# Top-k attention and mixture of depths on one core: score blocks turned by half rows, and a new order of signs, exponentials and loads

## The chip, the core and the metric

The kernel runs on one core of one Trainium2 chip. The metric is the device time in microseconds of one execution; a version is represented by the median of several runs. Engines are called by the names that the profile gives them: PE (matrix products; PEld is its loading of weights), DVE (VectorE), ACT (ScalarE), POOL (GpSimd) and SP (which here only issues DMAs).

## What is computed

Two operators follow one another. The first is attention with 8 batches, 8 heads, 576 tokens and 64 elements a head, in which each row keeps only its 32 largest scores:

```python
scores = scale * np.matmul(q, k.transpose(0, 1, 3, 2))
kth = np.partition(scores, -top_k, axis=-1)[..., -top_k:-top_k + 1]
scores = np.where(scores >= kth, scores, -1000000000.0)
attn = softmax(scores)            # over the keys
x = np.matmul(attn, v)            # then heads side by side: (8, 576, 512)
```

The second, the mixture of depths, works on each batch: a gate `x @ w_gate` for every token, and for the 128 tokens with the largest gates `x + sigmoid(gate) * (relu(x @ w1) @ w2)`, with w1 of 512 x 1024; all other tokens keep x.

## The kernel before

**Units and steps.** Work is cut into 144 units, 18 to a batch. A unit is 128 query rows of two heads; the last 64 rows of a batch are laid out so that four heads share one unit. One pass of the loop at L1108 is called a step here. It is a software pipeline written out by hand: step n computes the scores of unit n + 1, finds a bound for unit n, the signs for unit n - 1, the exact threshold for unit n - 2, the mask for unit n - 3, and turns, exponentiates and multiplies unit n - 4 with the values. Each engine runs its instructions in the order in which the program issues them (`InOrder`, L37), so the order of the lines in the loop sets every queue.

**What a step does, engine by engine, in the order of the code.**

1. `weigh` (L1053) turns unit n - 4: `turn` (L621) takes the 128 x 576 scores of each of two heads in four blocks of 128 keys. For each of these eight blocks PE makes a transpose (a product with `ident`, FP32) into the PSUM tile `ptr` (two banks), and then adds a second product, of the 0/1 matrix `less` (BF16) with `out_of_reach` (a diagonal of very negative numbers), which pushes every score below the threshold out of the reach of the exponential. `turn_last` (L630) does the same for a ninth block, the last 64 keys of both heads together, into a corner of the PSUM bank `av`. Then ACT makes the exponentials: `pT` (128 x 1024) and `last` (128 x 128).
2. `mask_of` (L1102) makes `less` for unit n - 3: the first head on ACT, the second on POOL. `flush` issues small pieces of ACT work put off from the step before.
3. The scores of unit n + 1: first one or two load pieces (`load[0]`, transposes of rows of k and q for the next batch, whose issue also fetches a further piece by DMA on SP's queue), then `multiply` (L486): eight products of 64 x 128 weights and 288 columns into `ps` (four banks); the two heads lie on rows 0 to 63 and 64 to 127 of the array. ACT copies the load pieces (`load[1]`) and then the scores (`keep`, `sc`).
4. `values` (L642) multiplies `pT` and `last` with the values into the bank `av`; ACT copies the result (`xs`). Then follow, on PE, pieces of an earlier batch's mixture, which `next(mixtures[b])` issues at the end of a step at times listed by hand (`mix_at`, L1001).
5. DVE: `find_bound` (L520) takes the 8 largest of each of 14 pieces of a row and sifts them to a lower bound of the threshold. In the middle of it stand delayed pieces of work; `gates` makes the gate by a dot product (`prod`, 40 in all). Then `find_kth` (L573) takes the 8 largest of `y` (tile `next`), whose last is the exact threshold.
6. `what_is_below` (L1072), the last in the step: for each head ACT takes the sign of the score against the bound and sums it (`part`, L554, tile `sides`), POOL multiplies scores and signs (`y`), and `fill` adds 8 columns that depend on the count.

**Buffers.** There are five `sc`, two each of `sides`, `y`, `less` and `pT`, and one each of `ptr`, `av` and `ps`. PSUM has eight banks, all in use.

**After the loop** the last four units are weighed by `weigh_unit` and `values_unit` (L1241 to L1248) with more PSUM room, among the last batch's mixture. A general path at the end of the program, for inputs that the fast path can't treat, isn't entered here.

Of the kernel before, what the change touches and what calls it, by code (L numbers as in the profile page):

```python
# [48 lines left out]
def kernel(  # L49
# [160 lines left out]
    def flush():  # L210
        while late:
            late.pop(0)()
# [24 lines left out]
    class Rows:  # L237
# [88 lines left out]
        def turn(self, i, tr, c0=0, c1=J):  # L326

            for c in range(c0, c1):
                pe.transpose(
                    tr[:, c - c0, :],  # L330
                    self.rows[i][:, c, :, :].rearrange("p h d -> p (h d)"),
                    ident,
                )
            if c1 == J:
                self.fetch()
# [144 lines left out]
    def room_for_scores():  # L480
        return ps_sc.tile([P, 2, 2, 512], FP32, name="ps")
# [126 lines left out]
    def turn_some(tr, z, less):  # L608

        pe.transpose(tr, z, ident)  # L610
        if less is not None:
            pe.matmul(
                tr, less, out_of_reach, start=False, stop=True, skip_group_check=True
            )

    def room_to_turn():
        return ps_tr.tile([P, 2, J, P], FP32, name="ptr"), ps_av.tile(
            [P, 512], FP32, name="av"
        )

    def turn(z, tr, less=None):  # L621

        for i in range(2):
            for c in range(J):
                at = slice(c * P + i * R, (c + 1) * P + i * R)
                turn_some(
                    tr[:, i, c, :], z[:, i, at], None if less is None else less[:, i, at]
                )

    def turn_last(z, av, less=None):  # L630

# [10 lines left out]
    def values(t, g, pT, last, av, vs):  # L642

        vt, vpair = vs  # L650
        for i, heads in enumerate(heads_of(t, g)):
            for c in range(J):
                for r in (0, R):
                    h = heads[-1 if r else 0][0]
                    pe.matmul(
                        av[r : r + R, i * DE : (i + 1) * DE],
                        pT[:, i, c, r : r + R],
                        vt[:, h, c, :],
                        start=(c == 0 and i == 0),
                        stop=False,  # L660
                        skip_group_check=True,
                    )
        for r in (0, R):
            h = heads_of(t, g)[0][-1 if r else 0][0]
            pe.matmul(
                av[r : r + R, 0 : 2 * DE],
                last[:, r : r + R],
                vpair[:, h // 2, :, :].rearrange("p h e -> p (h e)"),
                start=False,
                stop=True,  # L670
                skip_group_check=True,
            )
# [373 lines left out]
    inverting = normalised = None  # L1046
    of_batch = {}
    scs, bounds, ys, next8s, masks = {}, {}, {}, {}, {}

    def is_unit(n):  # L1050
        return 0 <= n < N

    def weigh(sc, tr, av, less):  # L1053

        turn(sc, tr, less)
        tr_last = turn_last(sc, av, less)
        pT = ptpool.tile([P, 2, J, P], FP32, name="pT")
        last = ptpool.tile([P, P], FP32, name="last")

        def exp():  # L1060
            act.activation(pT, tr, AF.Exp, scale=scale)
            act.activation(last, tr_last, AF.Exp, scale=scale)

        return pT, last, exp

    def bound_of(n):
        b, i = divmod(n, per_batch)
# [2 lines left out]
        find_bound(scs[n], bounds[b][:, i, :, :])  # L1070

    def what_is_below(n):  # L1072
        at, sc = 2 * n, scs[n]
        b, i = divmod(n, per_batch)
        bound = bounds[b][:, i, :, :]
        sides = wkpool.tile([P, 2, S], BF16, name="sides")
        y = wkpool.tile([P, 2, S + 8], FP32, name="y")
        for i in range(2):
            part(i, sc, bound, at, sides)
            pool.tensor_tensor(y[:, i, 0:S], sc[:, i, :], sides[:, i, :], ALU.mult)  # L1080
        fill(y, at)
        ys[n] = y

    def kth_of(n):
# [23 lines left out]
    for n in range(-1, N):  # L1108
        b, i = divmod(n, per_batch)
        if i == 0 and 0 <= b < B - 1:  # L1110
            qkv[b + 1] = room_for_qkv(b + 1)
            loading = chain(
                loading, Rows(k[b + 1], q[b + 1], *qkv[b + 1][0:2]).parts()
            )
        if 0 < n + 1 < NHP:
            first_pairs.turn(n + 1)
        if n == 0:
            for hp in range(2):
                first_pairs.turn_queries(hp)
            for hp in range(2):  # L1120
                first_pairs.keep_queries(hp)
        if n == NHP - 1:
            for hp in range(2, NHP):
                first_pairs.turn_queries(hp)
            for hp in range(2, NHP):
                first_pairs.keep_queries(hp)
            first_pairs.last_queries()
            first_steps.close()
            ps_sc = all_steps.enter_context(
                tc.tile_pool(name="ps_sc", bufs=1, space=PS)  # L1130
            )
        if n == 1:
            load_v(v[0], qkv[0][2])
        if n == NHP:
            load_weights()


        gating = normalised
        if inverting is not None:
            normalised = inverting[0:2]  # L1140
            vector_late.insert(0, lambda a=inverting: normalise(*a))
            inverting = None
        else:
            normalised = None
        if gating is not None:
            amid_late.append(lambda a=gating: gates(*a))

        if is_unit(n - 4):  # L1150
            tr, av = room_to_turn()
            pT, last, exp = weigh(scs.pop(n - 4), tr, av, masks.pop(n - 4))
            exp()
        if is_unit(n - 3):
            mask_of(n - 3, (act, None) if n in scatter_steps else None)
        flush()
        if is_unit(n + 1):
            b, t, g = units[n + 1]
            kT, qT = qkv[b][0:2]
            b, i = divmod(n, per_batch)  # L1160
            if n + 1 < NHP:
                ps = room_for_first_scores()
                multiply(t, g, kT, qT, ps)
                if is_unit(n - 1):
                    what_is_below(n - 1)
                stay_busy((10, 10, 20, 30)[n + 1])
            else:
                ps = room_for_scores()
                loads = list(islice(loading, first_loads[i] if b == 0 else loads_at[i]))
                halves = [ps[:, a, :, HALF : HALF + P] for a in range(2)]  # L1170
                for load, half in zip(loads, halves):
                    load[0](half)
                multiply(t, g, kT, qT, by_head(ps))
                for load, half in zip(loads, halves):
                    load[1](half)
                if n == NHP - 1:
                    stay_busy(20)
            scs[n + 1] = keep(ps)
        if is_unit(n - 4):
            b4, t4, g4 = units[n - 4]  # L1180
            values(t4, g4, pT, last, av, qkv[b4][2])
            if n in place_steps:
                values_bank[0] = av
                next(mixtures[place_steps[n]])
            if g4 == 0:
                xs = xpool.tile([P, H, DE], FP32, name="xs")
                if t4 == 0:
                    x = xpool.tile([P, NT, HD], FP32, name="x")
                    pg = gates_of[b4 % 2]
                    of_batch[b4] = x, pg  # L1190
            keep_values(t4, g4, av, xs)
            if g4 == groups(t4) - 1:
                inverting = b4, t4, xs
                n4 = R if t4 == J else P
                keep_sums(n4, xs, sums[0:n4, b4 * NT + t4, :])
            while kept:
                kept.pop(0)()


        if is_unit(n):  # L1200
            bound_of(n)
        flush_vector()
        flush_pool()
        if is_unit(n - 2):
            kth_of(n - 2)
        while after_kth:
            after_kth.pop(0)()


        if is_unit(n - 1) and n + 1 >= NHP:  # L1210
            what_is_below(n - 1)

        if gating is not None:
            b, t = gating
            if t == J:
                store(out[b], of_batch[b][0])
                mixtures[b] = mixture(float(b * S), of_batch[b][1], ranks[:, b, :])
        for b in mix_steps.get(n, ()):
            next(mixtures[b], None)
        b, i = divmod(n, per_batch)  # L1220
        if i == v_at and 0 <= b < B - 1:
            load_v(v[b + 1], qkv[b + 1][2])
# [17 lines left out]

    def weigh_unit(m):  # L1241
        tr, av = other_room(m) if (N - m) % 2 else room_to_turn()
        weighed[m] = *weigh(scs.pop(m), tr, av, masks.pop(m)), av

    def values_unit(m):
        pT, last, _, av = weighed[m]
# [371 lines left out]
```

## Time and profile before

| | |
|---|---|
| median of 3 runs | 814.45 us (814.24 to 816.94) |
| the profiled execution | 816.28 us, of which the span of the profile is 814.4 us |
| granted TensorE clock | 0.998 |
| DVE busy | 783.5 us (96% of the span) |
| PE busy | 777.2 us (95%); PEld 600.3 us (74%) |
| ACT busy | 729.5 us (90%) |
| POOL busy | 721.6 us (89%) |
| PE's `ptr` transposes | 1136, mean 280 ns |
| PE's `ptr` mask products | 1136, mean 219 ns |
| ACT `sides` | 288, mean 791 ns |

Matmuls are pipelined: the 280 ns of one is the time from its start to the end of its drain, and the next one starts long before that. For PE one therefore reads the distances between starts in the timeline, not the durations. Idle time is given with what ended it ("releaser"); a timeline line has the start and the length in us, the engine, the line, the operation, what it writes and reads, the shape and how many were merged. "128\*64" is the shape of the weights, rows by columns. All kernel work stands under one line, L45, so tiles are the names to go by. The units before step 35 or so have no mixture beside them; the last batches have a denser one.

### The profile page before, as it was taken

Reading aid. Unit: us, or ns where it says so; the run is one execution under the profiler, and the core shown is the slowest. Engines: PE = TensorE matmul, PEld = TensorE weight load, DVE = VectorE, ACT = ScalarE, POOL = GpSimd, SP = SyncE. Lnnn points to the kernel's source line nnn. Section 1 sums busy time; section 2 is a strip of 40 time slices with the busy share of each in tenths; the row PEclk is TensorE's granted clock in tenths of the full one; section 3 lists DMA queues with packets and bytes.
Section 4 is the critical chain, followed back from the end, with each engine's and each line's share of the span. In section 5 each row is a group of like instructions: output and inputs, shape, how many; then the busy total and the mean of one; then the engine's idle time right before and its main releaser. Section 6 shows DMA issues by size and latency. Waiting matters only on the chain. (4 is left out here: it accounts for less than half of the span.)

```text
span 814.4 us, 28453 instructions
## 1 busy us (share of the span) xinstructions
PE 777.2 (95%) x10231; PEld 600.3 (74%) x10231; DVE 783.5 (96%) x4655; ACT 729.5 (90%) x1577; POOL 721.6 (89%) x722
## 2 busy tenths in 40 slices
PE   8988888888999999999999999999999999999987
PEld 6766666667887778877787777877788777867756
DVE  6999999999999999999999999999999999999962
ACT  5999999999999999999999999999999999879840
POOL 3899999999999999999999999999999999998921
PEclk9999999999999999999999999999999999999999
DMA  8931214121151123221251221512224102001021
GB/s 169 287 89 28 52 58 106 29 53 28 60 114 26 43 59 90 66 54 33 74 106 29 54 41 60 100 28 54 41 80 94 28 3 79 23 5 25 2 72 30
DMA packets 121732, 50.38 MB, mean 62 GB/s; under 512 B 116016, under 2 KB 116016, under 8 KB 120560
## 3 DMA queue, kind: packets, MB, share of 16 engines
q1 hardware_dynamic: 118368, 43.94, 22.0%
q0 software_dynamic: 1744, 4.20, 2.9%
q8 instruction: 82, 1.34, 0.7%
q14 instruction: 66, 0.54, 0.2%
q10 hardware_dynamic: 1472, 0.36, 0.2%
HBM read 36.93 MB, written 11.55 MB: 60 GB/s over the span
## 5 line engine op out<-in xcount | busy, mean ns | idle before, releaser
L45 POOL TENSOR_TENSOR y<-sc,sides 128x576 f32<-128x576 f32 x288 | 365.8, 1294 | 51.0 <-ACT sides L45 49.3
L45 DVE MAX8 cand<-sc 128x8 f32<-128x82 f32 (+1 forms) x2016 | 314.0, 227 | 4.3 <-ACT sc L45 4.2
L45 POOL TENSOR_SCALAR less<-sc,next 128x576 bf16<-128x576 f32 x135 | 233.2, 1728 | 2.2 <-DVE next L45 1.2
L45 ACT ACTIVATE sides<-sc,bound 128x576 bf16<-128x576 f32 x288 | 223.5, 791 | 0.0
L45 PE MATMUL ptr<-out_of_reach,less 128*128 128x128 bf16 x1136 | 203.3, 219 | 18.0 <-POOL less L45 17.1
L45 PE MATMUL ptr<-ident,sc 128*128 128x128 f32 x1136 | 214.6, 280 | 0.0
L45 DVE MAX8 next<-y 128x8 f32<-128x584 f32 x288 | 204.4, 751 | 0.5 <-POOL y L45 0.5
L45 PEld LDWEIGHTS av<-v,pT 128*64 128x64 f32 x4608 | 146.1, 137 | 65.9 <-ACT last L45 62.6
L45 ACT ACTIVATE pT<-ptr 128x1024 f32<-128x1024 f32 x142 | 145.3, 1024 | 39.5 <-PE ptr L45 38.5
L45 PEld LDWEIGHTS ptr<-ident,sc 128*128 128x128 f32 x1136 | 159.9, 141 | 28.2 <-issue 16.7
L45 PE MATMUL ps<-kT,qT 64*128 64x288 f32 (+1 forms) x1248 | 174.0, 425 | 0.0
L45 PE MATMUL av<-v,pT 128*64 128x65 f32 x4608 | 166.0, 224 | 8.1 <-ACT last L45 7.4
L45 PEld LDWEIGHTS <-less 128*128 128x128 bf16 x1296 | 134.4, 104 | 36.7 <-POOL less L45 24.0
L45 ACT COPY sc<-ps 128x1152 f32<-128x1152 f32 x140 | 159.1, 1137 | 0.0
L45 PEld LDWEIGHTS ps<-kT,qT 64*128 64x128 f32 (+1 forms) x1248 | 95.8, 175 | 34.5 <-issue 20.9
L45 ACT ACTIVATE less<-sc,next 128x576 bf16<-128x576 f32 x141 | 109.8, 779 | 2.9 <-DVE next L45 2.8
L45 DVE MATCH_REPLACE8 cand<-best,cand 128x21 f32<-128x21 f32 (+1 forms) x576 | 98.9, 179 | 0.0
L45 DVE MAX8 best<-cand 128x8 f32<-128x21 f32 (+1 forms) x576 | 90.3, 189 | 0.0
L45 PE MATMUL h_ps<-xeT,w 128*128 128x128 f32 x464 | 65.7, 286 | 0.0
L45 PEld LDWEIGHTS h_ps<-xeT,w 128*128 128x128 f32 x464 | 55.8, 191 | 9.1 <-issue 7.0
L45 ACT ACTIVATION_READ_ACCUMULATOR sides<-sc,bound 128x1 f32 x288 | 61.0, 212 | 0.0
L45 PE MATMUL y_ps<-w,hT 128*128 128x512 f32 x112 | 60.6, 636 | 0.0
(165 smaller groups left out, 908.3 us busy)
## 6 DMA issues: line engine op xcount, KB each, us to landing
v<-in_v_dram SPq DMA_DIRECT2D x64, 128.0 KB, 4.4
out_dram<-x SPq DMA_DIRECT2D x8, 1024.0 KB, 4.0
rows<-in_k_dram SPq DMA_DIRECT2D x56, 128.0 KB, 2.9
rows<-in_q_dram SPq DMA_DIRECT2D x56, 128.0 KB, 3.0
w<-in_moe_w_dram SPq DMA_DIRECT2D x2, 2048.0 KB
gate_row<-row_dram SPq DMA_DIRECT2D x7, 288.0 KB, 4.4
last<-in_q_dram SPq DMA_DIRECT2D x8, 128.0 KB, 3.3
vpair<-in_v_dram SPq DMA_DIRECT2D x16, 64.0 KB, 3.9
```

The lines of the kernel that those rows point to most:

```text
L45: return lambda *a, **kw: self._tc.keep_in_program_order(fn(*a, **kw))
```

## The change

Four things are rearranged; no step of the computation goes or comes.

- `turn` makes each block in two halves of 64 query rows: a transpose of rows 0 to 63 and one of rows 64 to 127 (each 64 rows by 128 keys, against a 64 x 64 corner of `ident`), then the two mask products likewise. The two halves lie in different PSUM banks: `by_half` gives `ptr` (and `pT`) the layout half, block, row in place of head, block, row, and `values` reads `pT` accordingly.
- In the loop, the scores of unit n + 1 now come right behind the eight blocks. The ninth block, its exponential and the load pieces come behind the scores.
- The signs of unit n - 1 go on ACT from the end of step n to its beginning: the first head's right behind the exponential `pT`, the second's behind the exponential `last`. POOL's products `y` stay where they were (`weigh_signs`).
- `less` of unit n - 3 and the delayed ACT work come behind these.

After the loop, `weigh_unit` uses the halves as well and keeps its order otherwise.

```diff
     def turn(z, tr, less=None):
 
+        to = by_half(tr)
+        halves = [slice(r * R, (r + 1) * R) for r in range(2)]
         for i in range(2):
             for c in range(J):
                 at = slice(c * P + i * R, (c + 1) * P + i * R)
-                turn_some(
-                    tr[:, i, c, :], z[:, i, at], None if less is None else less[:, i, at]
-                )
+                for r, q in enumerate(halves):
+                    pe.transpose(to[:, r, i * J + c, :], z[q, i, at], ident[q, q])
+                for r, q in enumerate(halves):
+                    if less is not None:
+                        pe.matmul(
+                            to[:, r, i * J + c, :],
+                            less[q, i, at],
+                            out_of_reach[q, q],
...
-                        pT[:, i, c, r : r + R],
+                        by_half(pT)[:, r // R, i * J + c, :],
...
         if is_unit(n - 4):
             tr, av = room_to_turn()
-            pT, last, exp = weigh(scs.pop(n - 4), tr, av, masks.pop(n - 4))
+            pT, last, exp, turn_rest = weigh(scs.pop(n - 4), tr, av, masks.pop(n - 4))
             exp()
-        if is_unit(n - 3):
-            mask_of(n - 3, (act, None) if n in scatter_steps else None)
-        flush()
+        early = is_unit(n - 1) and n + 1 >= NHP
+        if early:
+            sign(n - 1, 0)
         if is_unit(n + 1):
...
                 ps = room_for_scores()
+                multiply(t, g, kT, qT, by_head(ps))
+        if is_unit(n - 4):
+            turn_rest()()
+        if early:
+            sign(n - 1, 1)
+        if is_unit(n - 3):
+            mask_of(n - 3, (act, None) if n in scatter_steps else None)
+        flush()
+        if is_unit(n + 1):
+            if n + 1 >= NHP:
+                b, i = divmod(n, per_batch)
                 loads = list(islice(loading, first_loads[i] if b == 0 else loads_at[i]))
                 halves = [ps[:, a, :, HALF : HALF + P] for a in range(2)]
                 for load, half in zip(loads, halves):
                     load[0](half)
-                multiply(t, g, kT, qT, by_head(ps))
                 for load, half in zip(loads, halves):
                     load[1](half)
...
-        if is_unit(n - 1) and n + 1 >= NHP:
-            what_is_below(n - 1)
+        if early:
+            weigh_signs(n - 1)
```

Here `sign(n, i)` is one `part` (one ACT sign with its sum), `weigh_signs(n)` POOL's two products and the `fill`, and `turn_rest` PE's ninth block followed by the exponential `last`.

More of the change, by code (lines that the diff above doesn't have):

```diff
@@ L619, in room_to_turn, with by_half @@
         )
+    def by_half(a):
+        return a.rearrange("p r c (b i) -> p r (c b) i", i=R)
     def turn(z, tr, less=None):
+        to = by_half(tr)
+        halves = [slice(r * R, (r + 1) * R) for r in range(2)]
         for i in range(2):
@@ L625, in turn @@
                 at = slice(c * P + i * R, (c + 1) * P + i * R)
-                turn_some(
-                    tr[:, i, c, :], z[:, i, at], None if less is None else less[:, i, at]
-                )
+                for r, q in enumerate(halves):
[6 more added lines that the diff above has]
+                            out_of_reach[q, q],
+                            start=False,
+                            stop=True,
+                            skip_group_check=True,
+                        )
     def turn_last(z, av, less=None):
@@ L1048 @@
     scs, bounds, ys, next8s, masks = {}, {}, {}, {}, {}
+    sides_of = {}
     def is_unit(n):
@@ L1055, in weigh @@
         turn(sc, tr, less)
-        tr_last = turn_last(sc, av, less)
         pT = ptpool.tile([P, 2, J, P], FP32, name="pT")
@@ L1061, in exp, with turn_rest @@
             act.activation(pT, tr, AF.Exp, scale=scale)
-            act.activation(last, tr_last, AF.Exp, scale=scale)
-        return pT, last, exp
+        def turn_rest():
+            tr_last = turn_last(sc, av, less)
+            return lambda: act.activation(last, tr_last, AF.Exp, scale=scale)
+        return pT, last, exp, turn_rest
     def bound_of(n):
@@ L1072, in what_is_below, with sign, weigh_signs @@
     def what_is_below(n):
[L1073 to L1076, printed above, removed]
+        for i in range(2):
+            sign(n, i)
+        weigh_signs(n)
+    def sign(n, i):
+        b, m = divmod(n, per_batch)
+        if i == 0:
+            sides_of[n] = wkpool.tile([P, 2, S], BF16, name="sides")
+        part(i, scs[n], bounds[b][:, m, :, :], 2 * n, sides_of[n])
+    def weigh_signs(n):
+        sc, sides = scs[n], sides_of.pop(n)
         y = wkpool.tile([P, 2, S + 8], FP32, name="y")
         for i in range(2):
-            part(i, sc, bound, at, sides)
             pool.tensor_tensor(y[:, i, 0:S], sc[:, i, :], sides[:, i, :], ALU.mult)
-        fill(y, at)
+        fill(y, 2 * n)
         ys[n] = y
@@ L1159 @@
             kT, qT = qkv[b][0:2]
-            b, i = divmod(n, per_batch)
             if n + 1 < NHP:
@@ L1242, in weigh_unit, with both @@
         tr, av = other_room(m) if (N - m) % 2 else room_to_turn()
-        weighed[m] = *weigh(scs.pop(m), tr, av, masks.pop(m)), av
+        pT, last, exp, turn_rest = weigh(scs.pop(m), tr, av, masks.pop(m))
+        exp_rest = turn_rest()
+        def both():
+            exp()
+            exp_rest()
+        weighed[m] = pT, last, both, av
     def values_unit(m):
```

## The prediction

> **What bounds it now.** I read the busy table by stretches first, then the waits of one batch, then the timeline of one step on TensorE (PE) and ScalarE (ACT). The stretch is one batch in the middle, 18 steps (columns: stretch, then busy us and instruction counts of PE, PE's weight loads, VectorE (DVE), ACT, GpSimd (POOL), clock, DMA).
>
> ```profile
> 330.75:426.67 95.92, 94.87 (x1264) 73.43 (x1263) 95.77 (x577) 91.07 (x198) 90.47 (x88) 1.00 0.27 61
> ```
>
> 95.92 / 18 = 5.33 us a step. DVE has no idle time and PE nearly none, at full clock; ACT and POOL have 5% each. The waits of that batch:
>
> ```profile
> PEld av L45 <- ACT last L45: 7.9, 17, 1.1
> POOL y L45 <- ACT sides L45: 4.9, 9, 0.8
> ACT pT L45 <- PE ptr L45: 4.7, 13, 0.6
> ```
>
> The first says that the value products wait for the exponential of the *last* block, which reads the bank (`av`) that they write. One step shows what that costs (ACT, then PE):
>
> ```profile
> 405.58 1.02 ACT L45 ACTIVATE pT<-ptr 128x1024 f32<-128x1024 f32 x1
> 406.50 0.27 ACT L45 ACTIVATE last<-av 128x128 f32<-128x128 f32 x1
> ...
> 409.01 0.82 ACT L45 ACTIVATE sides<-sc,bound 128x576 bf16<-128x576 f32 x1
> ...
> 409.78 0.81 ACT L45 ACTIVATE sides<-sc,bound 128x576 bf16<-128x576 f32 x1
> ...
> 410.69 1.02 ACT L45 ACTIVATE pT<-ptr 128x1024 f32<-128x1024 f32 x1
> ```
>
> ```profile
> 405.32 0.39 PE L45 MATMUL ps<-ident,rows 128*128 128x128 f32 x2
> 405.64 1.24 PE L45 MATMUL ps<-kT,qT 64*128 64x288 f32 x8
> 406.82 1.15 PE L45 MATMUL av<-v,pT 128*64 128x65 f32 x32
> 407.81 0.39 PE L45 MATMUL av<-vpair,last 128*64 128x130 f32 x4
> 408.13 1.16 PE L45 MATMUL h_ps<-xeT,w 128*128 128x128 f32 x8
> 409.13 0.27 PE L45 MATMUL ptr<-ident,sc 128*128 128x128 f32 x1
> 409.24 0.22 PE L45 MATMUL ptr<-out_of_reach,less 128*128 128x128 bf16 x1
> 409.29 0.28 PE L45 MATMUL ptr<-ident,sc 128*128 128x128 f32 x1
> ```
>
> There is a ring through ACT and PE: exponential pT, exponential last, values, the mixture's matmuls, the next turning, the next pT. Its least length here is 1.24 (pT start to values start) + 2.30 (values to turning) + 1.57 (turning to the next pT) = 5.11 us. Where last is not what values wait for, PE's own chain sets 5.33 (pT to values 1.46, PE without a gap). So three limits lie close together: the ring 5.1, PE 5.3, DVE 5.33 on the mean.
>
> **Part 1, turning by halves.** Eight blocks, each now two transposes on 64 rows and two mask products on 64 rows. Before, a block takes 409.29 - 409.13 = 0.17: 0.115 transpose, 0.055 mask. Do two row halves run side by side? The scores do, in this very mode (64*128): 8 products of 288 columns take 1.08 to the end of streaming, while 288 columns at the 0.112 per 128 of the h products would be 0.25 each, 2.0 in all. What does a half cost? The loads' last rows are turned with 64 rows and 64 columns, all in one half:
>
> ```profile
> 399.93 0.40 PE L45 MATMUL ps<-ident,last 64*128 64x64 f32 x3
> ...
> 400.17 0.22 PE L45 MATMUL ps<-ident,last 64*128 64x64 f32 x1
> ```
>
> The third of these starts at 399.93 + 0.40 - 0.22 = 400.11, the fourth 0.06 later. So a half transpose takes 0.06 with its weight load, and a half mask product streams in under 0.03, but the next weights must come in behind it, about 0.057 (the weight loads of these rows start that far apart). With both halves side by side a block takes 0.06 + 0.058 = 0.118. If nothing overlaps it takes 0.235; if streaming alone counted, 0.085. I take 0.118, nearest to the rows. Turning to pT: seven blocks of 0.118, 0.06 into the eighth, 0.23 from its last mask product to pT (0.26 now, on 128 columns), and 0.06 for a first load not fetched ahead: 1.17 instead of 1.57.
>
> The Trainium skill ("TensorE: Matmul & The Clock Gate", section "LDWEIGHTS (loading the stationary operand)") speaks against this part: a weight load goes by its columns, at columns / 1.2 ns, whatever the rows, so 107 ns for each half as for the whole. By that rule a block would be about 0.163, the step 0.32 longer and the kernel some 33 us slower than I forecast. The 0.06 spacing above is a 128-column load and its transpose together, so the row decides.
>
> **Part 2, modes on PE.** Each change of the array's shape costs: from the second load transpose (405.32 + 0.39 - 0.27 = 405.44) to the scores is 0.20 where the same mode repeats in 0.115, so 0.09, and then a first load that was not ahead. Before, scores are entered from the full shape; after, they follow the half turning without a change, and the last block and the load transposes (full shape) come behind the scores. What is new is the entry from the mixture into the half turning, 0.09 (plus the 0.06 counted above). PE's own chain falls by 0.42 - 0.20 + 0.30 changes, net to about 5.0: no longer a bound. The load transposes' DMA fetches move some 1.2 us later in SP's queue; they land in 2.9 us and are fetched two pieces ahead, so they are hidden; without that cover the next load transposes would wait those 1.2 us, in the 16 steps a batch that have one.
>
> **Part 3, the order on ACT.** Per step: pT, sign, last, sign, less, load copies, scores copy, xs. Nothing is added, and POOL's own order (less, x, y, y, fill) stays. But one sign now stands between pT and last: a sign takes 0.77 to the next start (409.78 - 409.01), so last starts 0.92 + 0.77 = 1.69 after pT instead of 0.92, and values start 0.32 after that: 2.01 instead of 1.24. PE has the last block ready at about 1.3 (scores 1.05, change 0.15, block 0.17, drain 0.2, from a turning that ended 0.23 before), so ACT sets it. Queued behind last: the value products, everything of PE behind them, the next turning. This is the new critical wait.
>
> Gains of part 3: POOL gets its signs 3 us earlier, so it follows DVE's `next` instead of the signs. This matters to DVE through its dot (`prod`), which slows when POOL is in a `y`:
>
> ```profile
> 93.43 1.75 DVE L45 CUSTOM_DVE_ANT_0 prod<-x,wg 128x512 f32<-128x512 f32 x1
> ```
>
> ```profile
> 93.36 2.97 POOL L45 TENSOR_TENSOR y<-sc,sides 128x576 f32<-128x576 f32 x2
> ```
>
> Without overlap with a y it is 0.68 (the one at 190.14); the 40 take 42.2 in sum, so at most 42.2 - 40 x 0.68 = 15 us are there. After, POOL's less starts no earlier than DVE's step and lasts 1.72, the dot starts 1.3 into the step, and the y come behind: nearly all dots fall to 0.68.
>
> **The sum.** The ring after: 2.01 + (values to turning, as before) + 0.09 + 1.17. The mean from values to turning is 2.22 in the four batches from 235 to 618 us, 2.42 in the denser one to 716, 2.68 in the ten steps to 772; 2.30 in the six steps ahead of 235. That gives 5.49 x 18 = 98.8 against 95.9: +2.95 x 4 = 11.8; 102.4 against 97.2: +5.2; 59.5 against 56.1: +3.4; 33.4 against 31.9: +1.5. Together +21.9. Ahead of step 34 (203 us) the ring is short (2.01 + 1.31 + 0.09 + 1.17 = 4.6, no mixture), DVE stays the bound, and its eight dots fall from 10.45 to 5.44: -5.0. ACT can enter the mixtures some 1 us further ahead of DVE, and of the last scores' margin at the end another 1 to 2 us is consumed before DVE stops: about -2.5. The last four units' turning is faster too, but DVE is busy there: 0 (were DVE not the cover, 4 x 0.4 = 1.6). Net +14. The profiled execution took 816.28 (span 814.4), so it would be about 830; the runs' median 814.45 gives **828**.
>
> **Rivals.** (a) *Faster*, DVE stays the bound: the half turning streams without waiting for weights (block 0.085), ring 5.26. From a ring of 5.35, that is a block of 0.098, this case decides. Then the dots' 15 us are the gain, less what the last ones have already: about 801. For: DVE has no idle time today; against: the 0.06 row. (b) *Even*: the block near 0.10, or values' wait partly hidden; 811 to 818. (c) *Halves do not overlap* when they alternate transposes and mask products, so the change doesn't do what it says: loads one after the other give 0.17, +0.36 x 104 steps (34 to 137), 866; nothing side by side gives 0.235, some 920 with the early steps bound too. Against: the scores' overlap. (d) *Values need only pT*, not last: ring under 5.0, again 801. Against: 17 waits on last in one batch.
>
> **Numbers.** A change of 0.5% (4 us, about what a measurement of this kernel can tell) separates the cases. Forecast (818.5 to 842) 0.58; (c) 0.13, so slower 0.71; (b) 0.12; (a) and (d) 0.17. The forecast's own bounds: a block 0.01 either way is 7 us, a mode change 0.05 either way 5 us. The range 805 to 845 leaves out the fastest of (a), the slow end and (c), under 2 in 10.
>
> **What would show it.** Right: PE's wait for last grows from 62.6 to over 90 us, values start 2.0 after pT, POOL's wait for sides (49.3) nearly gone, DVE waiting for `sc` (4.2 now) by 15 to 25 us, `prod` near 0.7, half turning 1.2 us to pT. Wrong: DVE still without idle time; or a block of 0.17 and more; or values starting before last.

## The result, and the profile after

The changed kernel takes **853.85 us** (median of 4 runs, 852.36 to 853.9) against 814.43 for the kernel before (4 runs, 814.24 to 816.94). The ratio is 1.047, with a 95% interval of 1.045 to 1.050: slower, as forecast, but by 39 us instead of 14, and outside the range. The profiled execution took 853.87 us, its span is 852.0 us at a granted clock of 0.996.

The table by stretches, for one middle batch of 18 steps (from the pT exponential of unit 58 to that of unit 76, as before):

```profile
334.31:436.42 102.11, 91.75 (x1551) 66.96 (x1551) 96.99 (x576) 90.92 (x198) 88.41 (x88) 1.00 0.24 57
```

A step takes 102.11 / 18 = 5.67 us instead of 5.33. DVE, which had next to no idle time before (0.15 us a batch), now idles 5.1 us a batch, and PE 10.4 us. The waits of that batch say who is waited for:

```profile
ACT pT L45 <- PE ptr L45: 11.5, 18, 1.2
PEld av L45 <- ACT last L45: 11.4, 18, 0.9
...
POOL out_dram L45 <- DVE next L45: 4.9, 1, 4.9
DVE cand L45 <- ACT sc L45: 4.4, 8, 1.0
...
PEld h_ps L45 <- ACT hT L45: 1.7, 3, 0.6
```

Two waits occur in all 18 steps: ACT waits for the turning, and PE for `last`. That is the ring of the prediction, closed. DVE waits for the scores' copy. Two lines were not foreseen: POOL's scatter (`out_dram`) waits 4.9 us, and PE's h products (the mixture's first matrix product) wait for `hT`, a relu on ACT. One step on ACT, then on PE:

```profile
413.39 1.03 ACT L45 ACTIVATE pT<-ptr 128x1024 f32<-128x1024 f32 x1 [0.24 <-PE ptr L45]
414.31 0.77 ACT L45 ACTIVATE sides<-sc,bound 128x576 bf16<-128x576 f32 x1
...
415.07 0.27 ACT L45 ACTIVATE last<-av 128x128 f32<-128x128 f32 x1
415.23 0.77 ACT L45 ACTIVATE sides<-sc,bound 128x576 bf16<-128x576 f32 x1
...
415.99 0.77 ACT L45 ACTIVATE less<-sc,next 128x576 bf16<-128x576 f32 x1
416.65 0.37 ACT L45 ACTIVATE hT<-h_ps 128x256 f32<-128x256 f32 x1
```

```profile
415.39 1.15 PE L45 MATMUL av<-v,pT 128*64 128x65 f32 x32 [0.45 <-ACT last L45]
416.37 0.39 PE L45 MATMUL av<-vpair,last 128*64 128x130 f32 x4
417.08 1.16 PE L45 MATMUL h_ps<-xeT,w 128*128 128x128 f32 x8 [0.32 <-ACT hT L45]
418.17 0.28 PE L45 MATMUL ptr<-ident,sc 64*128 64x64 f32 x2
```

Values start 415.39 - 413.39 = 2.00 us after pT, and the next pT (419.35) comes 1.18 after the turning starts: both as forecast. But the values-to-turning stretch is 418.17 - 415.39 = 2.78, because the h products stand idle until `hT` is there. `hT` is one of the delayed pieces that `flush` issues. In the changed order it is behind both signs and `less`, and ends 3.63 us after pT starts.

Where the 37.6 us between the two profiled spans lie, read from the starts of the pT exponential of each unit in the traces:

| stretch | before | after | difference | forecast |
|---|---|---|---|---|
| start to unit 34 | 203.0 | 197.5 | -5.5 | -5.0, and a part of -2.5 |
| units 34 to 40 | 31.9 | 34.7 | +2.8 | +1.5 |
| units 40 to 112 (four batches) | 383.6 | 408.4 | +24.9 | +11.8 |
| units 112 to 130 | 97.2 | 105.9 | +8.7 | +5.2 |
| units 130 to 138 | 44.1 | 48.4 | +4.3 | +3.4 (for ten units) |
| unit 138 to the end | 54.7 | 57.1 | +2.4 | the rest of -2.5 |

### The profile page after: what moved, and what is told of

Same layout as the page of the kernel before. It is cut to its first block, busy times and chain, and to the rows that moved or that the text cites. A ratio compares the mean times of both kernels' runs of the same rounds, so it can differ in the third digit from the quotient of the medians.

```text
span 852.0 us, 33323 instructions
## 1 busy us (share of the span) xinstructions
PE 748.0 (88%) x12535; PEld 552.3 (65%) x12535; DVE 785.3 (92%) x4655; ACT 728.3 (85%) x1577; POOL 708.8 (83%) x722
## 5 line engine op out<-in xcount | busy, mean ns | idle before, releaser
L45 POOL TENSOR_TENSOR y<-sc,sides 128x576 f32<-128x576 f32 x288 | 378.2, 1387 | 44.0 <-ACT sides L45 43.0
L45 DVE MAX8 cand<-sc 128x8 f32<-128x82 f32 (+1 forms) x2016 | 315.6, 229 | 35.2 <-ACT sc L45 33.2
L45 POOL TENSOR_SCALAR less<-sc,next 128x576 bf16<-128x576 f32 x135 | 245.3, 1817 | 25.8 <-DVE next L45 20.5
L45 PEld LDWEIGHTS av<-v,pT 128*64 128x64 f32 x4608 | 146.4, 137 | 95.3 <-ACT last L45 94.6
L45 PE MATMUL ps<-kT,qT 64*128 64x288 f32 (+1 forms) x1248 | 170.9, 423 | 10.3 <-ACT sc L45 10.1
L45 PEld LDWEIGHTS ptr<-ident,sc 64*128 64x128 f32 x2272 | 137.5, 137 | 47.4 <-issue 40.7
L45 PEld LDWEIGHTS <-less 64*128 64x128 bf16 (+1 forms) x2448 | 158.0, 129 | 8.6 <-POOL less L45 7.9
L45 PE MATMUL ptr<-ident,sc 64*128 64x64 f32 x2272 | 158.8, 252 | 0.0
L45 PE MATMUL ptr<-out_of_reach,less 64*128 64x64 bf16 x2272 | 146.0, 190 | 6.2 <-POOL less L45 5.8
L45 PEld LDWEIGHTS ps<-kT,qT 64*128 64x128 f32 (+1 forms) x1248 | 93.1, 176 | 31.3 <-ACT sc L45 14.4
L45 ACT ACTIVATION_READ_ACCUMULATOR sides<-sc,bound 128x1 f32 x288 | 57.8, 201 | 0.0
```

Source lines behind the costliest of these rows:

```text
L45: return lambda *a, **kw: self._tc.keep_in_program_order(fn(*a, **kw))
```

## The experiments

The theory to test is that the ring's terms are as forecast, and that one more term counts, which the prediction had at nothing: the delayed pieces behind signs and `less`. Rivals: the signs' place itself costs more than the ring says; or the delayed pieces don't matter and PE's new order does. The mean lengths of the ring's three parts in the middle batch, from the traces, are given here once for all kernels (us). Each part goes from start to start: of the first transpose of a turning, of the exponential pT, and of the first product of pT with the values.

| kernel | turning to pT | pT to values | values to turning | step |
|---|---|---|---|---|
| before | 1.69 | 1.42 | 2.22 | 5.33 |
| after | 1.24 | 2.00 | 2.43 | 5.67 |
| x1, delayed pieces right behind last | 1.22 | 2.00 | 2.31 | 5.53 |
| x2, signs back at the end | 1.48 | 1.51 | 2.31 | 5.30 |
| x3, x1 with whole blocks | 1.60 | 2.00 | 2.22 | 5.82 |
| x4, only the halves | 1.49 | 1.48 | 2.31 | 5.28 |
| x5, x1 with both signs ahead of last | 1.17 | 2.75 | 2.31 | 6.23 |
| x6, x1 with last in the scores' banks | 1.47 | 1.44 | 2.33 | 5.25 |
| x7, both signs behind last | 1.36 | 1.77 | 2.31 | 5.44 |
| x8, x6 with the delayed pieces late | 1.35 | 1.38 | 2.63 | 5.36 |
| x9, x7 with last in the scores' banks | 1.74 | 1.49 | 2.31 | 5.54 |
| x10, x6 with the signs at the end | 1.82 | 1.19 | 2.31 | 5.32 |
| x11, x9 with less ahead of last | 1.43 | 1.43 | 2.39 | 5.25 |

The three parts always add up to the step (but for rounding). What tells a closed ring is that all three stand at their least length in nearly every step, as in after, x1, x3 and x5; in before, x2, x4, x6, x10 and x11 the slack moves between them and DVE sets the step: DVE has 0.14 to 0.15 us of idle time in the whole batch there.

**x1: the delayed pieces alone.** In the loop of the changed kernel:

```diff
             turn_rest()()
+        flush()
         if early:
             sign(n - 1, 1)
         if is_unit(n - 3):
             mask_of(n - 3, (act, None) if n in scatter_steps else None)
-        flush()
```

> The changed kernel with ScalarE's delayed pieces (relu of h, copies for the mixture) issued right behind the exponential last, ahead of the second sign and of less. Theory (ring plus a late delayed piece): relu of h now ends 2.2 us after pT's start instead of 3.6, so the h products no longer wait; values to turning is 2.39 in every h step (now 2.39 and 2.78 in turn), the mean step of a middle batch falls from 5.67 to 5.50, and the kernel to 828 to 835. Rival 1 (half turning itself costs): stays at 850 to 856. Rival 2 (the scores copy stands too late in ScalarE's order): the order ahead of that copy holds the same work, so 850 to 856.

Measured 838.12 us (836.91 to 840.44), ratio to before 1.029 (1.026 to 1.031): 16 us of the loss are gone, a little fewer than expected. Page rows of after and of x1, for the h products; the last column is the idle time ahead of them:

```profile
L45 PE MATMUL h_ps<-xeT,w 128*128 128x128 f32 x464 | 66.7, 289 | 9.9 <-ACT hT L45 6.3
```

```profile
L45 PE MATMUL h_ps<-xeT,w 128*128 128x128 f32 x464 | 66.4, 288 | 0.0
```

The wait is gone, and values to turning is 2.31: the 2.22 of before and the 0.09 for the change of shape that the prediction added. Of the 25 us by which four batches grew, 10.2 were the late pieces (408.4 against 398.3 in x1).

**x2: signs back.** Both signs at the end of the step again (`what_is_below(n - 1)` in place of `weigh_signs(n - 1)`, both `sign` calls dropped), everything else as in after.

> The changed kernel with both signs back at the end of the step; halves, last block and loads behind the scores stay. Theory: last starts 1.3 after pT (PE is what it waits for), values 1.6, ring 1.6 + 2.4 + 1.17 = 5.2, below VectorE's 5.33, so VectorE is the bound again: 808 to 817. Rival 1 (half turning itself costs): 840 or more. Rival 2 (scores copy too late): about 814, since the copy is early again.

Measured 816.57 us, ratio 1.001 (1.000 to 1.002). The signs' place, with what it pushes back, is 37 of the 39 us. The delayed pieces are behind `less` here too, but two signs earlier, and values to turning stays at 2.31. The 2 us that are left hide two larger terms, which x4 tells apart.

**x4: the halves alone**, in the old order (`turn` and `values` of after in the kernel before).

> The kernel before with nothing changed but the turning by halves (signs, last block and loads where they were). Theory: turning to pT 1.17 instead of 1.57, two changes of mode more, PE's chain about 5.2, VectorE the bound: 808 to 816. Rival 1 (half turning itself costs): 840 or more. Rival 2 (scores copy too late): about 814.

Measured 808.16 us, ratio 0.992 (0.990 to 0.994): a gain of 7 us for part 1 by itself. DVE is the bound here as it was before, and the gain lies in its dots: 36.4 us in sum against 42.2. x2 has the same halves, the same order on ACT and the signs in the same place; it differs from x4 only in PE's order, with the scores ahead of the ninth block and the load pieces. It is 8.4 us slower (816.57 against 808.16), 5.1 of it in the dots (41.5). So without early signs the new order on PE takes back what the halves gain.

**x3** is the reverse of x4, whole blocks in x1's order:

> As the run with the delayed pieces first, but the eight blocks turned whole (128 rows) as in the kernel before; signs, last block and loads as changed. Theory (ring): turning to pT 1.57 instead of 1.17, one change of mode (0.09) less, so +0.3 in each of 104 steps: 838 becomes 865 to 875. The halves are then the good part of the change. Rival 1 (half turning itself costs, for its twofold count of instructions): 838 or less.

Measured 867.36 us (one run), 29 above x1. The step is 5.82 = 1.60 + 2.00 + 2.22: turning costs what it did, 0.38 more than by halves, and the 0.09 for the change of shape is gone, so the step is 0.28 longer than in x1, 5.1 a batch.

**x5: two signs ahead of last** (`sign(n - 1, 1)` moved up behind `sign(n - 1, 0)`, else x1).

> As the run with the delayed pieces first, but both signs stand between pT and last (the suspected cost doubled). Theory (ring): pT to values 2.77 instead of 2.0, step 6.3 in the mixtures and 5.3 ahead of them: 910 to 930. Rival 2 (the scores copy too late in ScalarE's order): the same work stands ahead of the copy, so 838 as in that run.

Measured 922.82 us (one run). pT to values goes from 2.00 to 2.75: a sign ahead of `last` costs 0.75 of its 0.77 us in each step, nothing of it is hidden.

**x6: values made free of last.** x1, with the ninth block turned by halves into unused columns of the scores' banks, so that `last` no longer reads the bank that values write:

```diff
+    def turn_last_halves(z, ps, less):
+        to = ps[:, :, 0, HALF + P : HALF + P + R]
...
-            turn_rest()()
+            exp_rest = turn_rest(ps if is_unit(n + 1) else None)
+        if is_unit(n + 1) and n + 1 >= NHP:
...
+                load[0](half)
+        if is_unit(n - 4):
+            exp_rest()
+        flush()
```

> As the run with the delayed pieces first, and the last block turned by halves into spare columns of the scores' banks instead of the bank that the values are written to. ScalarE's order is the same. Theory: values no longer wait for last, only the last four products of them do; they start 1.5 after pT, ring 5.1, VectorE the bound with most dots at 0.68: 798 to 812. Rival 2 (scores copy too late in ScalarE's order): as slow as that other run, 828 or more. Rival 1: 828 or more.

Measured **801.73 us** (801.25 to 803.93), ratio 0.984 (0.982 to 0.986): faster than both kernels. Its batch by stretches:

```profile
322.47:416.95 94.48, 91.46 (x1587) 69.18 (x1587) 94.34 (x576) 91.04 (x197) 88.27 (x88) 1.00 0.27 63
```

In the first step of this batch pT starts at 322.47, values 1.40 later and ahead of `last`. On PE and on ACT:

```profile
323.87 1.16 PE L45 MATMUL av<-v,pT 128*64 128x65 f32 x32
```

```profile
324.15 0.27 ACT L45 ACTIVATE last<-ps 128x128 f32<-128x128 f32 x1
```

DVE is busy in 94.34 of 94.48 us, so the step is now DVE's own work, and the sum of all 40 dots is 28.6 us (42.2 before, 35.7 after). The order of the change pays once the ring is cut.

**x10: the same with the signs at the end.** x6 and this differ in the signs' place alone.

> As the version with the last block in the scores' banks and the delayed pieces ahead of the second sign (801.7), but with both signs back at the end of the step, so that only the signs' place differs. Theory (the early signs pay through DVE's dots, up to 15 us of them): dots of 0.7 to 1.8 us come back, their mean rises from 0.68 to about 0.9, 8 us: 805 to 815, DVE without idle time. Rival (with the ring out of the way, the place of the signs is free): 799 to 803.

Measured 813.96 us (812.31 to 815.19), ratio 0.998 (0.997 to 0.999). The dots are back at 40.4 us. So early signs are worth 12 us (813.96 - 801.73), almost all in the dots (40.4 - 28.6 = 11.8), which is what part 3 of the prediction hoped for.

**x8: x6 with the delayed pieces late**, `flush` as in after.

> The last block in the scores' banks (the run of 801.7), but with the delayed pieces where the change has them, behind the second sign and less. Theory: relu of h ends 3.6 after pT while the h products could start 3.0 after it, so +0.6 in every other h step (4 a batch), part of it taken up by PE's slack, and the scatter of an earlier batch waits for its gy on GpSimd once a batch: 803 to 812. If the delayed pieces cost nothing outside the ring: 800 to 803.

Measured 820.3 us (819.17 to 827.73): a miss, 19 us over x6 where up to some 10 were expected. The late pieces hurt even with values free of `last`: in every second h step the h products wait, in sum 21.2 us before their matmuls, and values to turning is 3.38 to 3.70 where they wait for `hT` and 2.40 in the h steps between (in after 2.78 and 2.40). The wait is 1.0 to 1.3 us, since values start earlier here (on the mean 1.38 after pT instead of 2.00) while `hT` still ends 3.63 after pT. The profiled execution is the longest of the five (827.73 us), and one dot in it takes 6.63 us, so its sums stand above those of a usual one.

**x7: both signs behind last**, delayed pieces between pT and `last`, the ninth block in `av` as in after.

```diff
-        if early:
-            sign(n - 1, 0)
+        flush()
...
             turn_rest()()
         if early:
+            sign(n - 1, 0)
             sign(n - 1, 1)
```

> The changed kernel with ScalarE's order pT, delayed pieces, last, sign, sign, less, copies; last stays in the values' bank. Theory (ring): last is ready 1.3 after pT, values start 1.6, ring 5.2, VectorE the bound, dots near 0.68 as the signs are early: 799 to 808. Rival 2: the scores copy is as late as in the changed kernel, so 838 or more.

Measured 834.83 us, ratio 1.025 (1.023 to 1.027): a miss by 27 us. The ACT timeline shows a hole in each step without a delayed piece to fill it:

```profile
324.57 1.02 ACT L45 ACTIVATE pT<-ptr 128x1024 f32<-128x1024 f32 x1
326.05 0.28 ACT L45 ACTIVATE last<-av 128x128 f32<-128x128 f32 x1 [0.45 <-PE av L45]
```

Steps ahead of the mixtures, where the ring of the prediction is short, take 5.4 on the mean as well (units 8 to 34). I took it for ACT's queue, too long by a hole; the next run tests that.

**x9: x7's order with x6's banks**, so that the ninth block is ready earlier.

> The last block by halves into spare columns of the scores' banks, and ACT's order: pT, delayed pieces, last, both signs, less, copies. With the same order and the last block in av ACT idled 0.45 us a step ahead of last (44.0 us in sum) and its own queue of 5.38 us was the bound. Theory (that idle time was the price, not the order as such): the last block now needs no change of shape behind the scores, so it is ready about 1.25 instead of 1.48 us after pT starts; ACT's queue falls to about 5.15, under DVE's 5.25, and DVE is the bound: 799 to 807, ACT's wait for last about half of 44 us, the dots near 0.68. Rival 1 (signs behind last are late for POOL, and the order costs by itself): 825 to 836. Rival 2 (ACT's wait does not shrink): 830 to 836.

Measured 852.11 us (849.29 to 854.81): far off, 17 slower than x7, though values no longer wait for `last`. PE and ACT of one step:

```profile
337.01 1.24 PE L45 MATMUL ps<-kT,qT 64*128 64x288 f32 x8 [0.26 <-ACT sc L45]
...
338.14 0.20 PE L45 MATMUL ps<-out_of_reach,less 64*128 64x64 bf16 x2
338.26 0.44 PE L45 MATMUL ps<-ident,rows 128*128 128x128 f32 x2
```

```profile
338.74 0.28 ACT L45 ACTIVATE last<-ps 128x128 f32<-128x128 f32 x1 [0.69 <-PE ps L45]
...
341.35 1.12 ACT L45 COPY sc<-ps 128x1152 f32<-128x1152 f32 x1
```

This is another ring, through the scores' single buffer `ps`: scores start when ACT's copy of the ones before has ended; `last` starts when the products behind the scores have ended (338.70; it waits for the load transposes too, which write the same tile); behind it on ACT stand two signs, `less`, a load copy and the scores' copy, which ends at 342.47. From 337.01 that is 5.5 us. In x7, where `last` reads `av` and doesn't wait for the load transposes, the same chain is 0.14 shorter: 5.38. ACT's hole is its symptom. For x9 the next run tests this; for x7 it is read from the timeline alone.

**x11: x9 with ACT's `less` ahead of last.** The `mask_of` lines move from behind the signs to directly behind pT.

> As the version with the last block in the scores' banks and both signs behind last (852), but with ACT's less moved ahead of last, so that ACT's order is pT, less, delayed pieces, last, sign, sign, load copies, scores copy, xs. Theory (a ring through the scores' single buffer: scores 1.07, last block and load transposes up to last 0.66, last 0.17, two signs 1.52, less 0.66, load copy 0.25, scores copy 1.12, next scores 0.05: 5.5 us as measured; the idle time of ACT ahead of last is its symptom): with less out of it the ring is 4.84, ACT's queue of 5.06 us has no hole left, and DVE is the bound: 798 to 808, ACT's wait for last under 15 us. Rival 1 (it is the signs' place behind last, late for POOL, that costs): 835 to 852. Rival 2 (less ahead of last only moves the hole, to a wait for DVE's next): 815 to 835.

Measured 805.31 us (803.58 to 806.04), ratio 0.989 (0.987 to 0.990). With 0.66 us out of that ring, 47 us are gone, and ACT's wait for `last` falls from 66.5 to 1.7 us. Both signs are behind `last` in both kernels, so that place doesn't cost by itself; the ring through `ps` does.

## Why the prediction was wrong, step by step

- **Part 1 (a block of 0.118): right.** From the second block on, two transposes and two mask products repeat every 0.118; behind the two transposes at 418.17 come

```profile
418.29 0.19 PE L45 MATMUL ptr<-out_of_reach,less 64*128 64x64 bf16 x2
418.31 0.25 PE L45 MATMUL ptr<-ident,sc 64*128 64x64 f32 x2
...
418.43 0.25 PE L45 MATMUL ptr<-ident,sc 64*128 64x64 f32 x2
```

  Turning to pT is 1.17 where nothing else is late. x3 and x1 differ in the blocks alone, and this part is 1.60 with whole ones and 1.22 with halves. By the Trainium skill's rule on weight loads ("TensorE: Matmul & The Clock Gate", section "LDWEIGHTS (loading the stationary operand)") the block had been estimated at 0.163; the measured 0.118 decides against it here.
- **Part 2 (0.09 for entering the half shape): right.** Values to turning is 2.22 with whole blocks (x3) and 2.31 with halves (x1).
- **Part 3, the critical wait: right in place and size.** Values start 2.00 after pT against 2.01 forecast, in nearly all mixture steps. With a second sign ahead of `last` it is 2.75 (x5). PE's wait for `last` (the PEld rows) is 94.6 us, forecast over 90, and 3.9 in x6. DVE's wait for `sc` is 33.2 us, above the forecast 15 to 25 (23.8 in x1).
- **Part 3, "Nothing is added": this is the step that failed.** The order I wrote down for ACT, "pT, sign, last, sign, less, load copies", leaves out the delayed pieces, which the diff moves behind `less`. In the sum this became "values to turning, as before". It is 2.43 on the mean instead of 2.31: five steps of a middle batch take 2.75 to 2.98 where x1 has 2.36 to 2.40, four of them for want of `hT` and the fifth of another delayed piece, `xeT`. x1 undoes only this: from 853.85 to 838.12, which is inside the forecast range. POOL's scatter, once a batch, waits for another of these pieces (`gy`). On POOL and on ACT of after:

```profile
394.99 1.60 POOL L45 DMA_INDIRECT out_dram<-gy,row_i  x1 [4.87 <-DVE next L45]
```

```profile
394.03 0.68 ACT L45 ACTIVATE gy<-y_ps,g 128x512 f32<-128x512 f32 x1
```

  The profile names DVE's `next` here and ACT's `qT` in the same place of other batches. What holds in each of the middle batches is that the scatter starts 0.28 after its own input `gy` ends (394.71; in x1 the same, at 288.87 and 289.15). The products that `gy` reads had ended on PE at 389.66. The scatter's wait is 0.48 before, 3.45 in x1 and 4.87 in after, so most of it comes with the ring (it is 0.44 in x6, which has x1's order on ACT and no closed ring) and 1.4 us with the late pieces. POOL's `y` and `less` come late behind the scatter, and a later dot (at 408.05), which begins while POOL is in a `y` and goes on beside `less`, takes 2.19 us instead of 0.67; in x6 no dot takes more than 0.84.
- **The rest of the miss, 7 us by the profiled spans (x1 is +20.7 against +14 forecast; by the medians it is 838.12 against 828, so 10), has two parts.** Four batches grew by 14.7 in x1 instead of 11.8: in the one step of a batch without products of a mixture the ring is short and ACT's own queue sets it (5.26 us without idle time, 390.76 to 396.02 in after), so the turning stands ready for 0.8 us. I had worked with a mean ring and no such floor. The other part is the end: from unit 138 on x1 takes 2.0 us more than before, where I had counted on a head start. Its cause was not tried and stays open.
- **Dots: half right.** The first stretch gained 5.5 us, as forecast, 4.35 of it in its eight dots (10.45 to 6.10). The mean of all 40 is 0.89 (1.06 before), not near 0.7. That a dot takes 0.68 without a `y` beside it was read from one dot; others of the kernel before that meet `less` alone take 0.95 (147.2), 0.82 (168.6) and 1.16 (724.0), and five of the eight early dots of after take 0.81 to 0.83 beside `less`. And "POOL's wait for sides nearly gone" was wrong: it is 43.0 us (49.3 before), 29.7 in x1, and falls to 12.7 in x6, without the closed ring.
- **Rivals.** (b), (c) and (d) are out by the rows above: the block is 0.118, not near 0.10 and not 0.17, nothing of the sign ahead of `last` is hidden, and values do wait for `last`; (a), DVE as the bound, is what x6 shows, at the price worked out there (801), after the ring is cut in another way.

## What to carry to other kernels

When a line is moved in a hand-ordered program, list every call that lies between its old and its new place, helpers that issue delayed work above all: here one `flush()` that went along cost 16 of 39 us. When several limits lie at nearly the same length (5.1, 5.3 and 5.33 here), write down each ring with all its members on each in-order engine and every single buffer, because an edit that relieves one can lengthen the next, as x7 and x9 did. The order of the change was worth its trouble only after a dependence through one PSUM bank, which held the input of `last` and the result of the values in different columns, was taken out.

## What the hardware showed unasked

- The scores follow the half turning with hardly a gap: the last mask products start at 413.16 and the scores at 413.19 (after), where the kernel before needs 0.20 from its load transposes in the full shape to the scores.
- In x9 `last` waits for the latest products into its tile, not for those into its own columns alone: in the step shown it starts 0.04 us after the load transposes into other columns have ended, 0.40 after its own block. So it is in all 106 steps with load transposes in which ACT waits for it; in the 13 without them it starts 0.04 after its own block.
- The name of a releaser can be that of whatever ended last: the scatter's wait carries the names of a DVE and of an ACT instruction in batches that are otherwise alike. Its distance to the end of its own input (0.28), the same in all of these, was the better guide.
